# Another order of the steps in all loops of an attention and MLP kernel

## Chip, cores and metric

The kernel runs on one core of a Trainium2 chip, in fp32. The metric is the device time of one execution in microseconds. Engines are named as in the profile: PE (TensorE, matmuls), PEld (its weight loads), DVE (VectorE), ACT (ScalarE), POOL (GpSimd) and SP (SyncE, which here only issues DMAs).

## What is computed

The reference runs a linear attention with a decaying state and feeds its output to an MLP with the exact GELU:

```python
for t in range(S):                                    # S = 768, B = 4, H = 8, head size 48
    cur = einsum('bhd,bhe->bhde', u[None] * kt, vt)
    y[:, :, t] = einsum('bhd,bhde->bhe', rt, state + cur)
    state = wt[:, :, :, None] * state + einsum('bhd,bhe->bhde', kt, vt)
x = y.transpose(0, 2, 1, 3).reshape(3072, 384)
h = x @ w_in                                          # 384 x 2048
g = 0.5 * h * (1.0 + erf(h / sqrt(2)))
out = g @ w_out                                       # 2048 x 384
```

The two weight matrices come in as 64-bit floats; the kernel makes fp32 of them on the chip.

## The kernel before

**Tiling.** The 3072 tokens are cut into eight units of 384 (four batches, two halves each; a second half takes over the state of the first). For each unit the attention gives `xT`, the transposed input of the MLP (three blocks of 128 channels), and the MLP gives 384 rows of the output. Unit 0's attention is done in two parts, of two head pairs each.

**Loops.** Loop x (0 to 7) does the rest of the attention of unit x, begins that of unit x+1, and does the MLP of unit x-1; loop 8 is the last MLP alone. All parts are Python generators that issue a few instructions per step. `PLAN[x]` is a string; each letter advances one generator by one step (L1255). When the string is used up, what is left of the generators is run to its end in a fixed order (L1257). So PLAN is the order in which every engine gets its instructions, and each engine takes its own in that order. The generators:

- `.` the products of the MLP (loop 0: the attention of unit 0's first part; loop 1: `first_mlp`, L1045, with plain matmuls, 16 of h, each followed by a gelu on ACT at L1053, and then the output);
- `s` the attention of unit x from where it was left (loop 0: unit 0's second part), `f` the first steps of the attention of unit x+1;
- `l` loads (SP): the next unit's r, k, w in nine parts and v; in loop 0 the first weight pieces W0 to W2 and the shares of unit 1's input;
- `x` the 11 sums of blocks of xT (`sums_of_x`, DVE, L1036) that the fast product needs; in loop 0 two groups of three warm-up matmuls that keep PE busy (`keep_warm`, L349);
- `v` merges of product results (POOL's accumulating DMAs, L1115, or DVE, L1117 and L1120), `g` the gelus (ACT, L1133), `o` the 30 sums behind the output products (DVE, L1161 to L1168), `e` their 12 copies (ACT, L1084);
- `c` the conversion of one of 16 weight pieces, in four steps: prepare (three ACT operations, L457, L458, L460; two pieces ahead), shift (DVE, L469), nothing, add (DVE, L473) with the load of the piece three further on; `p` (loop 0) prepare for W1 and W2 apart; `w` the load of v for unit 1 (loop 0) and sums of weight blocks (loops 1 and 2); `y` sums of output weights (loop 1).

**The MLP (units 1 to 7)** makes both of its products by a scheme of 20 block products. The first is 2 x 20 steps of the list `STEPS` ("P3", "P12 se", ...; four matmuls each, L1040, with copies by ACT), the second 20 steps of two slots (`OUT_STEPS`). A step of the first list that opens a bank must wait until that bank is free. P17, the third of a loop, opens the bank (m0) that the previous MLP's accumulator D has left; D's last use is the sum "D-00", the last of the 30 in `OUT_SUMS`. The sums before it are A+10, A-00, N5-11, N5+10, M11N5, N4+12. In front of step O17 of the output stands the copy e11 (ACT), the last of `OUT_COPIES`.

**The attention of units 2 to 7** is 43 steps: the products ruk of r, u and k (DVE, L512); transposed sums TTR (L499); the running totals of w, tot (L532: the first two in one step, the rest in the next); products `apart` (L506) and `times` (L540); copies `plain` (ACT, L678) and `lay_out` (DVE, L683, L684); then per level (4 and 16) three bursts of 64x64 matmuls on PE (L708, the fine ones of level 4 at L700), here called d4.0 to d4.2 and d16.0 to d16.2, whose results are copied off the bank pairs by DVE (level 4, L737) or ACT (level 16, six copies, L724), with two bank pairs for three bursts; products of r and k (L753 to L764); the transposes trK (DVE, L657) with 12 DMAs on SP (L652), copies kt (ACT, L806), kv on PE (L822), the states st (DVE, L837), `inside` on PE (L863), a one-column copy named fence (DVE, L875) that PE waits for, y on PE (L908), the copy ysb (L934) with six DMAs, and six copies xT (ACT, L931). Units 0 and 1 use an older form of the middle part with six levels (`halves`, L590): bursts at L573 (level 1 with an additional one, diag), updates (DVE, L615 to L626), copies (DVE, L637, or for levels 16 and 32 ACT, L634), transposes ktT (L796), and products ru of r and u on ACT (L522). Unit 0's first part copies y straight into xT (L915, two copies on ACT, two on DVE).

The order stands in the code as these strings; the kernel has no planner and no due times.

Of the kernel before, what the change touches and what calls it, by code (L numbers as in the profile page):

```python
# [36 lines left out]
NC_SP = 8  # L37
HALFWAY = 2
PLAN = {
    0: ".xll.s...lcsl.ssslsslsls.l.slll..scls.ls.cpc.ss..csss..sscsl.sc...lsc.ssss.ls.l...sf.wfxpf",  # L40
    1: (
        "cl.c.cls.cccss.ccccwccwwc.sw.cccccsclcss.cc.llsscsc.cwccscs.cclsc.ccwscssw.c.wsscc.ccws.cl"
        "lcwwlcwwwsccw.cccsccs.cfcfcc..cl...fc.cfxcx..x.y..f.w....f.x.wy.y.wf.yw.yxy.xx...xywyw...."
        "yxyxwff.wxy"
    ),
    2: (
        ".l..w.wsw.sws..wv...ws..wvv..w.www.vlswwsg.wg..v.swsswswws.wlg..wl..g.s.wgv.vsvswv....ggwv"
        "s..g.vssvvssw..w.ssw.vvg.vvggs.g.vsggogg..eos.w..es..o..osso..eoo.e.o.ooooos..ewwle....eeo"
        "..soo.eo.esl..l.s.ooosoel..oeolslsw....fo.f.ooo.fox.oxxoxxxxxfxfxfx"
    ),  # L50
    3: (
        "....v.s....s....vvg.s.vs.vl.gs....g.s...ls.vg..sss.s.ssv.gs.vsgvs.svvv.vsg.ls.lgv.v.vvs.sg"
        "..gsggsv.gsg..sgg.eo.os..esos..so..oo.loe.eol.o..o.sooeoe..ee....oosesooss..lsel.l.ooosfes"
        "..o..folo.e.f.o.ox..oooxx..oxxxoxfxfxfxx"
    ),
    4: (
        ".ls.s......v..l.g.v..v...sg...vvl.g.v.s.sss..g.svss.vsss...s.ss.vvgvgvsg.glsg..vgss.vvv.v."
        "s.slv.sg.s.ggsglgog.s.e.o.s.eos....os.soooo.eoe....ooeooe...ee.o..sso.e.eoo.lss.lo.l.soeof"
        "sol..oefs..o..o.ofo..oofx.oxxoxxxxxfxfxx"
    ),  # L60
    5: (
        ".s.l..sv....s....v.sg..v..vg..vsl..lg.gvs.v.s..v.sss.vgsgss..s.gsvg.sv.lgssv..s.gs.v.vvv.s"
        ".sv.gvsgsggglgs..oos..es.e...o..os.l.sso.eoeo.s.oo.eeooo.o..e.eo.o..s.oo.sslee.osl.lof..se"
        "os..fl.ooeo..o.fofoo....xoxxooxxxfxxfxfxx"
    ),
    6: (
        "........s..vv......vg.sgs.v..gv..ssv.sv...s..sssvgss..vg.ssslvs.vg.s.vvg.sgl.gs.vv..vsvlgl"
        "s..gssggvsg..gog.s..eeo.s...o.ossso..ee...oooloeo.eolo..s.eo.o.oe..s.oe.o.elss..sooelo.lfs"
        ".o.eoflos....o.ofoof.oxo.x.xoxxxfxxfxfxx"
    ),  # L70
    7: (
        "ss......s.v...v..v.....g.vss...gvvg...s..v.gssg.gsssvs...s..vsgv.svggsvss..vs...vvgs.svvg."
        "ssg.gvsggg..ooesss....oeo.s.os..eo.e..oo.oooeo.oe....se.e.o.oes.oos...ess.osoeos...o.oo.e."
        "o.oo.ox.x.ooxxx.xoxxxxx"
    ),
    8: (
        "...........vv...vv.g..vvg.v..g....gv..v.vggg....gv....v.g.vg.vgvg.vgvv.g.g.g...o.eoe....oo"
        "..e.e...eooooeo....ooe.ooe..oo.oe..o..eoo..oo..oee....ooo.oo.o..oo"
    ),
}  # L80

# [1244 lines left out]
```

## Time and profile before

| | |
|---|---|
| time before, median of 3 runs | 589.58 us (588.73 to 589.81) |
| the profiled execution | 589.16 us |
| its span in the trace | 587.4 us, PE's granted clock 0.996 |
| PE, DVE, ACT, POOL busy | 555.5, 490.4, 330.8, 103.0 us |
| first matmul step of loops 1 to 8 | 49.2, 128.3, 192.9, 260.2, 327.9, 397.1, 462.6, 530.8 us |

In rows of the timeline the columns are: start in us, length in us, engine, line, operation, output and input tiles, shape, number of instructions taken together, and in brackets the idle time of the engine before it with what ended it. "issue" is idle time for which the trace shows no wait. In rows of waits the columns are the sum in us, how often, and the longest. Units are written as the loops: "loop 3" begins at 192.9 us. The trace's times start at the first instruction of the span.

### The profile page before, as it was taken

To read this page: it belongs to the slowest core of one execution; us is meant where nothing else is said; L and a number is where in the kernel's file an instruction comes from. 1 tells how busy PE (TensorE), PEld (TensorE's weight loads), DVE (VectorE), ACT (ScalarE), POOL (GpSimd) and SP (SyncE) were. 2 spreads that over 40 slices of the span, in tenths; PEclk is the share of its full clock that TensorE was granted. 3 is DMA by queue.
4 is the path that set the end of the run, shared out by engine and by line. 5 is a ranking of instruction groups with operands and counts; after the bars stand their busy time and mean duration, and the time that the engine had idled before them with its cause. 6 is when DMAs were issued, how large, how long until landed. Compare 5 with 4: busy or idle time off the path is not lost. (4 is left out here: it accounts for less than half of the span.)

```text
span 587.4 us, 17679 instructions
## 1 busy us (share of the span) xinstructions
PE 555.5 (95%) x7410; PEld 491.5 (84%) x7424; DVE 490.4 (83%) x997; ACT 330.8 (56%) x733; POOL 103.0 (18%) x99
## 2 busy tenths in 40 slices
PE   6769999999999999999998999989999899999997
PEld 3556666569999888999898889979899898989997
DVE  5959989998998989899897989789897989855464
ACT  2348999117862568437762577526772477625820
POOL 3100000005400351006400162003700072000000
PEclk8999999999999999999999999999999999999999
DMA  7829933126723583537813494327824375201001
GB/s 242 265 60 309 353 112 120 41 77 111 103 47 130 135 121 44 130 101 141 138 34 104 119 144 55 68 72 175 122 37 121 95 104 66 42 14 40 1 1 40
DMA packets 71646, 62.15 MB, mean 106 GB/s; under 512 B 32912, under 2 KB 56720, under 8 KB 71568
## 3 DMA queue, kind: packets, MB, share of 16 engines
q1 hardware_dynamic: 50256, 45.62, 25.7%
q0 software_dynamic: 21216, 15.34, 20.0%
q8 instruction: 58, 0.95, 0.7%
q14 instruction: 20, 0.16, 0.1%
q10 hardware_dynamic: 96, 0.07, 0.1%
HBM read 36.24 MB, written 4.72 MB: 70 GB/s over the span
## 5 line engine op out<-in xcount | busy, mean ns | idle before, releaser
L1115 POOL DMA_DIRECT2D g<-o_sb x78 | 95.0, 1504 | 378.5 <-ACT g L1084 312.5
L1164 DVE TENSOR_TENSOR g<-g 128x512 f32<-128x512 f32 x112 | 74.4, 686 | 21.8 <-PE o_ps L1040 19.2
L1084 ACT COPY o_sb<-u_ps 128x384 f32<-128x384 f32 (+1 forms) x56 | 25.6, 457 | 61.0 <-PE u_ps L1040 57.9
L1040 PE MATMUL h_ps<-forms_x,w_in_sb 128*128 128x192 f32 x280 | 58.0, 332 | 0.3 <-ACT g L1084 0.3
L1084 ACT COPY g<-h_ps 128x384 f32<-128x384 f32 x84 | 40.1, 479 | 18.5 <-PE h_ps L1040 16.7
L1040 PE MATMUL o_ps<-w_out_sb,g 128*128 128x192 f32 x280 | 50.1, 326 | 0.0
L1040 PEld LDWEIGHTS h_ps<-forms_x,w_in_sb 128*128 128x128 f32 x280 | 46.5, 190 | 3.1 <-ACT g L1084 2.1
L1133 ACT ACTIVATE g<-g 128x384 f32<-128x384 f32 x98 | 47.0, 521 | 0.7 <-DMA g<-o_sb 0.4
L1040 PEld LDWEIGHTS o_ps<-w_out_sb,g 128*128 128x128 f32 x280 | 46.1, 190 | 0.1
L1040 PE MATMUL o_ps<-t,g 128*128 128x192 f32 x224 | 41.4, 328 | 0.0
L724 ACT COPY a_sb<-d 32x320 f32<-32x320 f32 (+5 forms) x108 | 39.1, 362 | 3.2 <-DVE a_sb L782 1.0
L1040 PE MATMUL h_ps<-forms_x,s 128*128 128x192 f32 x168 | 36.1, 338 | 3.4 <-DVE o_sb L1167 3.3
L1040 PEld LDWEIGHTS o_ps<-t,g 128*128 128x128 f32 x224 | 36.8, 190 | 0.3
L1040 PE MATMUL h_ps<-xT,w_in_sb 128*128 128x192 f32 x168 | 35.0, 331 | 0.0
L1040 PEld LDWEIGHTS h_ps<-forms_x,s 128*128 128x128 f32 x168 | 27.4, 189 | 7.7 <-DVE o_sb L1167 4.7
L1051 PE MATMUL h_ps<-xT,w_in_sb 128*128 128x384 f32 x96 | 33.1, 495 | 0.2 <-ACT g L1053 0.2
L1040 PE MATMUL u_ps<-xT,w_in_sb 128*128 128x192 f32 x168 | 32.5, 329 | 0.2
L708 PE MATMUL d<-kx,rkw 64*64 64x96 f32 x1152 | 30.7, 247 | 1.8 <-DVE kx L684 1.6
L1040 PE MATMUL u_ps<-w_out_sb,g 128*128 128x192 f32 x168 | 31.1, 333 | 1.2 <-ACT u_ps L1084 1.2
L708 PEld LDWEIGHTS d<-kx,rkw 64*64 64x64 f32 x1152 | 25.3, 133 | 7.4 <-issue 3.6
L1059 PE MATMUL o_ps<-w_out_sb,g 128*128 128x384 f32 x96 | 31.4, 488 | 0.0
L837 DVE SCALAR_TENSOR_TENSOR st<-st,tot_sb,kv_ps 128x48 f32<-128x48 f32 x160 | 29.4, 258 | 1.2 <-PE kv_ps L822 1.1
(169 smaller groups left out, 1191.3 us busy)
## 6 DMA issues: line engine op xcount, KB each, us to landing
g<-o_sb POOLq DMA_DIRECT2D x78, 192.0 KB, 4.0
rkw<-in_rkw_dram SPq DMA_DIRECT2D x54, 256.0 KB, 3.4
raw<-in_w_out_dram SPq DMA_DIRECT2D x8, 768.0 KB, 5.6
v_in<-in_v_dram SPq DMA_DIRECT2D x8, 584.0 KB, 3.9
out_dram<-o_sb SPq DMA_DIRECT2D x24, 192.0 KB, 2.1
raw<-in_w_in_dram SPq DMA_DIRECT2D x5, 768.0 KB, 9.5
rkw<-kx SPq DMA_DIRECT2D x72, 48.0 KB, 2.0
rkw<-in_rkw_dram SPq DMA_DIRECT2D x6, 384.0 KB, 7.1
```

The lines of the kernel that those rows point to most:

```text
L708: nc.tensor.matmul(d[half[p], g, i * 3 * C // 2:(i + 1) * 3 * C // 2], lhsT=kc[half[g], n // NI, n % NI, p], rhs=rx[half[g], 2 * n + p], s ...
L724: nc.scalar.copy(out=at[z, g, first:behind, (a + 1) * h:], in_=d[z, :, :, to] if g == slice(None) else d[z, :, to])
L837: nc.vector.scalar_tensor_tensor(out=stq[:, q, c], in0=stq[:, q, c - 1] if c else b4[:, q, NC - 1], scalar=totq[:, q, c:c + 1], in1=kvs[q ...
L1040: nc.tensor.matmul(o, lhsT=lhsT, rhs=rhs, start=start, stop=True, skip_group_check=True)
L1051: nc.tensor.matmul(h_ps, lhsT=w_in_sb[:, f // FI, j, f % FI * 128:(f % FI + 1) * 128], rhs=xT[:, j, :], start=(j == 0), stop=(j == NJ - 1))
L1059: nc.tensor.matmul(o, lhsT=gs[f // FG][:, f % FG, i * 128:(i + 1) * 128], rhs=w_out_sb[:, f, :], start=(f == 0), stop=(f == NF - 1))
L1084: nc.scalar.copy(out=o, in_=z)
L1115: nc.gpsimd.dma_start(out=o, in_=saved[q, t], accum_op=ALU.add)
L1133: nc.scalar.activation(out=o, in_=z, func=AF.Gelu, scale=MINUS.get(h, 1.0))
L1164: nc.vector.tensor_add(o, o, g_block(what[3:5]))
```

## The change

Only the strings in PLAN change. Each loop keeps the number of every letter, apart from one step of `f` less in loop 0 (one step of `s` more in loop 1), one step of `f` more in loop 4 and one less in loop 5 (with one `s` less in loop 5 and one more in loop 6). In words, as far as it matters here:

- Loop 0: both groups of warm-up matmuls come at the very end (before: the first after the first step, the second at the end). The preparation of W1 comes behind the copies of levels 16 and 32 and kt (ACT); before, ahead of them. W0's shift and add come behind unit 0's level-32 update; before, among the levels. So W3's load comes later, too. The copies L915 come ahead of unit 1's ru and tot; before, behind them. The burst diag of unit 1 comes in loop 1, behind the first product of h; before, ahead of it.
- Loop 1: the conversions, levels of unit 1 and products of h alternate in other places; the gelu of h2 comes behind W4's preparation (before: ahead of it), that of h10 behind the level-16 copies (before: ahead).
- Loops 2 to 7: at the end of each loop fewer `x` steps come ahead of D-00 (loops 2, 4 and 6: one instead of three; loops 3 and 7: three instead of six; loop 5: three as before). In loops 4 and 6 the first two totals of the next unit come ahead of the sums N4+12 and M11N5; before, behind them. In loop 5 ruk of unit 6 comes behind the fence (before: ahead of it; in loops 4 and 6 it stays ahead).
- In loops 4 to 7 d16.2 comes right behind d16.1 and the product step P19 ahead of both; before, P19 and an output step stood between them. In loops 3 and 6 d4.0 comes one product step later.
- In all loops the letters `v`, `g`, `o`, `e` and `l` move by a few places; the order within each letter is the generator's and stays.

The diff (of the loops that aren't shown every line is replaced in the same way):

```diff
-    0: ".xll.s...lcsl.ssslsslsls.l.slll..scls.ls.cpc.ss..csss..sscsl.sc...lsc.ssss.ls.l...sf.wfxpf",
+    0: "l.s....llsl.lssslslss.lc.l.slslls...ssss..lcs.s.s.l.ss..ss..sccs.c.s.llpssslw..cs.ffpccxx",
     1: (
-        "cl.c.cls.cccss.ccccwccwwc.sw.cccccsclcss.cc.llsscsc.cwccscs.cclsc.ccwscssw.c.wsscc.ccws.cl"
-        "lcwwlcwwwsccw.cccsccs.cfcfcc..cl...fc.cfxcx..x.y..f.w....f.x.wy.y.wf.yw.yxy.xx...xywyw...."
-        "yxyxwff.wxy"
+        "l.ccswccclss.cw.l.ccccccscs.c.csscccc.scc.sscwccc.cswcs.wcsccscccls.c.ssc.sclcswcwcc.wcwcc"
+        "sslcw..cwlclwccswclsc.cf.w.cw..ccc.cfw..cfyx....f.x..x.f.yxxf.wxw..y..y...wywyx..xyxf.yw.f"
+        ".wxywxyl.yf."
     ),
...
     4: (
-        ".ls.s......v..l.g.v..v...sg...vvl.g.v.s.sss..g.svss.vsss...s.ss.vvgvgvsg.glsg..vgss.vvv.v."
-        "s.slv.sg.s.ggsglgog.s.e.o.s.eos....os.soooo.eoe....ooeooe...ee.o..sso.e.eoo.lss.lo.l.soeof"
-        "sol..oefs..o..o.ofo..oofx.oxxoxxxxxfxfxx"
+        "ls.....s.ss.v....g....vlv.s.gs.vv..g....sv...s.glssvvgsvslsss..gvs.v.gs.ggss..v.sgv.vv..vv"
+        ".slsggs.svsg.gog.g.s.oss.eo.e.o..o.so..ee..ooo..eoe.o..oosee.s..loo.os.oes.e.so.llsleo.of."
+        "s.o.esolo.f..f.ooo.o.foo..xoxxxxxxxffxfxx"
     ),
     5: (
-        ".s.l..sv....s....v.sg..v..vg..vsl..lg.gvs.v.s..v.sss.vgsgss..s.gsvg.sv.lgssv..s.gs.v.vvv.s"
-        ".sv.gvsgsggglgs..oos..es.e...o..os.l.sso.eoeo.s.oo.eeooo.o..e.eo.o..s.oo.sslee.osl.lof..se"
-        "os..fl.ooeo..o.fofoo....xoxxooxxxfxxfxfxx"
+        ".....sll....v....vv..vsg.vs....ggs.v..vs.ls..g.sv.ssssvs.sl..g.vs.vsvgs.s.ggv.gss..l..vsvv"
+        "vsssvg...ggsggogsg.os.oe.se.l.o..o..o.oe.es.o.oeeo....o..ooseoes..ose.loos.ssell..oo.eossf"
+        "..o..fo.oeof..o..xoo.oxox.oxxlxxxffxfxx"
     ),
...
```

More of the change, by code (lines that the diff above doesn't have):

```diff
@@ L39 @@
 PLAN = {
-    0: ".xll.s...lcsl.ssslsslsls.l.slll..scls.ls.cpc.ss..csss..sscsl.sc...lsc.ssss.ls.l...sf.wfxpf",
+    0: "l.s....llsl.lssslslss.lc.l.slslls...ssss..lcs.s.s.l.ss..ss..sccs.c.s.llpssslw..cs.ffpccxx",
     1: (
-        "cl.c.cls.cccss.ccccwccwwc.sw.cccccsclcss.cc.llsscsc.cwccscs.cclsc.ccwscssw.c.wsscc.ccws.cl"
-        "lcwwlcwwwsccw.cccsccs.cfcfcc..cl...fc.cfxcx..x.y..f.w....f.x.wy.y.wf.yw.yxy.xx...xywyw...."
-        "yxyxwff.wxy"
-    ),
-    2: (
-        ".l..w.wsw.sws..wv...ws..wvv..w.www.vlswwsg.wg..v.swsswswws.wlg..wl..g.s.wgv.vsvswv....ggwv"
-        "s..g.vssvvssw..w.ssw.vvg.vvggs.g.vsggogg..eos.w..es..o..osso..eoo.e.o.ooooos..ewwle....eeo"
-        "..soo.eo.esl..l.s.ooosoel..oeolslsw....fo.f.ooo.fox.oxxoxxxxxfxfxfx"
-    ),
@@ L51 @@
-    3: (
-        "....v.s....s....vvg.s.vs.vl.gs....g.s...ls.vg..sss.s.ssv.gs.vsgvs.svvv.vsg.ls.lgv.v.vvs.sg"
-        "..gsggsv.gsg..sgg.eo.os..esos..so..oo.loe.eol.o..o.sooeoe..ee....oosesooss..lsel.l.ooosfes"
-        "..o..folo.e.f.o.ox..oooxx..oxxxoxfxfxfxx"
-    ),
-    4: (
-        ".ls.s......v..l.g.v..v...sg...vvl.g.v.s.sss..g.svss.vsss...s.ss.vvgvgvsg.glsg..vgss.vvv.v."
-        "s.slv.sg.s.ggsglgog.s.e.o.s.eos....os.soooo.eoe....ooeooe...ee.o..sso.e.eoo.lss.lo.l.soeof"
-        "sol..oefs..o..o.ofo..oofx.oxxoxxxxxfxfxx"
-    ),
@@ L61 @@
-    5: (
-        ".s.l..sv....s....v.sg..v..vg..vsl..lg.gvs.v.s..v.sss.vgsgss..s.gsvg.sv.lgssv..s.gs.v.vvv.s"
-        ".sv.gvsgsggglgs..oos..es.e...o..os.l.sso.eoeo.s.oo.eeooo.o..e.eo.o..s.oo.sslee.osl.lof..se"
-        "os..fl.ooeo..o.fofoo....xoxxooxxxfxxfxfxx"
-    ),
-    6: (
-        "........s..vv......vg.sgs.v..gv..ssv.sv...s..sssvgss..vg.ssslvs.vg.s.vvg.sgl.gs.vv..vsvlgl"
-        "s..gssggvsg..gog.s..eeo.s...o.ossso..ee...oooloeo.eolo..s.eo.o.oe..s.oe.o.elss..sooelo.lfs"
-        ".o.eoflos....o.ofoof.oxo.x.xoxxxfxxfxfxx"
-    ),
@@ L71 @@
-    7: (
-        "ss......s.v...v..v.....g.vss...gvvg...s..v.gssg.gsssvs...s..vsgv.svggsvss..vs...vvgs.svvg."
-        "ssg.gvsggg..ooesss....oeo.s.os..eo.e..oo.oooeo.oe....se.e.o.oes.oos...ess.osoeos...o.oo.e."
-        "o.oo.ox.x.ooxxx.xoxxxxx"
-    ),
-    8: (
-        "...........vv...vv.g..vvg.v..g....gv..v.vggg....gv....v.g.vg.vgvg.vgvv.g.g.g...o.eoe....oo"
-        "..e.e...eooooeo....ooe.ooe..oo.oe..o..eoo..oo..oee....ooo.oo.o..oo"
+        "l.ccswccclss.cw.l.ccccccscs.c.csscccc.scc.sscwccc.cswcs.wcsccscccls.c.ssc.sclcswcwcc.wcwcc"
@@ new lines @@
+        "sslcw..cwlclwccswclsc.cf.w.cw..ccc.cfw..cfyx....f.x..x.f.yxxf.wxw..y..y...wywyx..xyxf.yw.f"
+        ".wxywxyl.yf."
+    ),
+    2: (
+        "s.w..s.w.w.s..w..wswv.w..v.ww.vwv.ssw.swgww.swgsvwv.w.sgwv.wssls..wvsw...wg...g...wvsw.gvl"
+        "s..sgvss...gg.ssvgvw.wvgvgvv.glsgv..gs.og.l.oe.s.wsoeo.s...seooe..l.so.ooe.lewo...o..ooeoe"
+        "..os.eolol.s.se..oo.oew.lsw.ooosles..f.fo.oo.o.fo..xooxxfxxxxxfxfxx"
+    ),
+    3: (
+        ".ls....v..s.sl...g...s.vvs..s..l.vg.gvg....s..l..sv.svss.ssss.g.svssgvlvg.sg..vv.vv.gsv.gv"
+        "s.sggv.gslsvs..g.ogsog.e..s.eoo.....seo.oe.os.eoo.e...oooso.e.e.s.soo.ool.lessseo..oeolssf"
+        "....fooo.e..f.xooxo.o..x.oooxlxxxfxfxfxx"
+    ),
@@ new lines @@
+    6: (
+        "s..sl...v.....v..g..ss.v.lvv...g.gvs..gsv..s.v..s.ssggsssvss..ss.l.vg.s..vg.vvggss..vvvv.."
+        "ssssvggg..g.so.ggsoe...seo...ssols.o.o.eooe...o.e.eo.o.o.e.ooeo..ssl.oos.lsel..eslooo..lef"
+        "s..oes.o.lfo..foo.o.o..fooxoxxxxxffxxxfxx"
+    ),
+    7: (
+        "....sv.......gss.v....vsv..g..sg..vvg..s...s.svsgvsvss.ss.ss.vvgs.v.gsg.vg..svg...vv.ssgsv"
+        "v.gg.g.sgso.gseo..es.....osso..ooo.eeoo..e.eso...oooee...os.soe..oos.se.s.oeosos...oo.e..."
+        "oooo..oxo.oxx.oxxxxxxxx"
+    ),
@@ L79 @@
+    8: (
+        "..........v...v...v.v..g.gggv.v.....vv.....g.gvg....vgv.vvvgvgv..vgg..g.vgo..gge..eo...o.o"
+        ".oo.eoe....oeo.e.o..o.oeeo..oo.eo.o.eo....ooe..o.e.oo.o..o.oo.oo.o"
     ),
```

## Prediction

> **What bounds the kernel now.** I read the page first: its line of busy times and PE's slices (busy tenths, 14.7 us each).
>
> ```profile
> PE 555.5 (95%) x7410; PEld 491.5 (84%) x7424; DVE 490.4 (83%) x997; ACT 330.8 (56%) x733; POOL 103.0 (18%) x99
> PE   6769999999999999999998999989999899999997
> ```
>
> TensorE (PE) is busy 95% of the span of 587.4 us; only slices 1 to 3, the first loop, hold clearly less. No edit changes its number of instructions, so the change can only move the 32 us in which PE is idle (587.4 - 555.5), and what it loses when it changes between kinds of work. The table of 50-us windows (length; PE, PEld, DVE, ACT, POOL busy; clock; DMA share; GB/s) says where those 32 us lie.
>
> ```profile
> 0.00:50.00 50.00, 35.43 (x1176) 26.11 (x1190) 36.80 (x113) 20.20 (x35) 8.00 (x21) 0.97 0.60 191
> 50.00:100.00 50.00, 49.35 (x886) 32.71 (x885) 46.20 (x80) 48.31 (x68) 0.00 (x0) 1.00 0.67 236
> 300.00:350.00 50.00, 46.94 (x589) 44.12 (x589) 41.83 (x90) 24.53 (x60) 10.36 (x9) 1.00 0.52 112
> 550.00:587.00 37.00, 33.87 (x208) 33.27 (x206) 19.40 (x38) 11.70 (x32) 0.00 (x0) 0.99 0.05 16
> ```
>
> 14.6 us are in the first 50 (loop 0 and its wait for the first loads) and 3.1 in the last 37 (mostly the last sums and store). The rest, about 14, lies in loops 2 to 7. Of that the waits of PE from 49 us on name this much:
>
> ```profile
> PE y_ps L908 <- DVE fence L875: 3.4, 4, 1.6
> PE h_ps L1040 <- DVE o_sb L1167: 3.3, 4, 1.1
> PE d L708 <- DVE kx L684: 1.6, 4, 0.6
> PE u_ps L1040 <- ACT u_ps L1084: 1.2, 2, 0.9
> PE kv_ps L822 <- DMA rkw<-kx: 1.0, 1, 1.0
> ```
>
> Each is a place where PE has come, in the order that PLAN fixes, to a step whose input is still queued on another engine behind steps that weren't urgent. Those are what another order can take away, so I price them one by one. In the first window and in the second ACT matters: 48.31 of 50 us busy, with the conversion of the weights.
>
> **Loop boundaries (P17).** Step P17, the third of a loop, needs the bank that D-00, the last of the 30 sums (L1167), gives back. PE's waits there:
>
> ```profile
> 195.36 0.92 PE L1040 MATMUL h_ps<-forms_x,s 128*128 128x192 f32 x4 [0.62 <-DVE o_sb L1167]
> 262.20 0.76 PE L1040 MATMUL h_ps<-forms_x,s 128*128 128x192 f32 x3 [0.56 <-DVE o_sb L1167]
> 330.46 0.92 PE L1040 MATMUL h_ps<-forms_x,s 128*128 128x192 f32 x4 [1.05 <-DVE o_sb L1167]
> 465.18 0.92 PE L1040 MATMUL h_ps<-forms_x,s 128*128 128x192 f32 x4 [1.03 <-DVE o_sb L1167]
> ```
>
> The sum is 3.26. Ahead of D-00 DVE does this in the third of them:
>
> ```profile
> 325.42 0.37 DVE L1161 TENSOR_TENSOR u_ps<-u_ps,o_sb 128x192 f32<-128x192 f32 x1 [0.89 <-PE u_ps L1040]
> 325.69 0.95 DVE L532 TENSOR_TENSOR tot_sb<-rkw 128x768 f32<-128x768 f32 x1
> 326.68 0.56 DVE L532 TENSOR_TENSOR tot_sb<-tot_sb 128x384 f32<-128x384 f32 x1
> 328.98 0.36 DVE L1036 TENSOR_TENSOR forms_x<-xT 128x192 f32<-128x192 f32 x1
> 330.06 0.34 DVE L1167 TENSOR_TENSOR o_sb<-o_sb,o_ps 128x192 f32<-128x192 f32 x1
> ```
>
> It idles 0.89 us for PE (first row) and only then does the two totals of the next unit (0.95 and 0.56 us, L532), which depend on no PE step. D-00 is the sum at 330.06. In the new order the totals stand ahead of the two sums N4+12 and M11N5 (at the boundaries from loop 4 to 5, this one, and from 6 to 7), so they fall into that idle time, and of the sums of x (L1036, 0.36 us in the fourth row) two fewer stand ahead of D-00, from loop 3 to 4 three fewer. Idle filled, 0.9, and two sums, 0.7, are more than the 1.05 and 1.03 waited; the 0.62 and 0.56 go by the two and three sums of x alone. I take all four as gone: **-3.26**. From 5 to 6, where PE now doesn't wait, four products ruk (L512) move from ahead of the fence to behind it: +0.3, an estimate (bounds 0 and 1.05, the largest of the rows above). In all **-2.96**. What is late next is the first burst of the loop, priced as unchanged below.
>
> **First bursts (d4.0).** Their input is DVE's L684.
>
> ```profile
> 213.65 1.88 PE L708 MATMUL d<-kx,rkw 64*64 64x96 f32 x80 [0.58 <-DVE kx L684]
> ```
>
> In loop 3 (first row; two bursts are taken together in it) the burst moves one PE step (0.65) later: **-0.5**. In loop 6 it does, too, but there ruk has moved behind the fence and DVE comes later by about as much; in loops 4, 5 and 7 it keeps its place, and PE and DVE come sooner by about the same. So the 1.0 left of the 1.6 stays. If DVE's idle isn't filled, the boundary waits come back here (first rival).
>
> **Loop 5's fence, and e11.**
>
> ```profile
> 384.62 3.03 DVE L512 SCALAR_TENSOR_TENSOR kx<-rkw,u_sb,rkw 128x384 f32<-128x384 f32 x4
> 387.72 0.99 PE L908 MATMUL y_ps<-rkw,st 64*64 64x64 f32 x51 [1.57 <-DVE fence L875]
> 393.11 1.08 PE L1040 MATMUL u_ps<-w_out_sb,g 128*128 128x192 f32 x5 [0.94 <-ACT u_ps L1084]
> ```
>
> In loop 5 the products (first row, 3.03 us) stand between the states and the fence, and PE waits 1.57 for it (second row). They move behind the fence; I leave 0.2 for the fence itself: **-1.37**. In loops 4 and 6 they stay ahead of it, so the rest of the 3.4 stays. y sooner makes its copy ysb and the six copies xT on ACT (L931) sooner; the copy e11, queued behind them, made PE wait 0.94 (third row). I leave 0.3: **-0.64** (bounds 0 and 0.94).
>
> **The wait for kv in loop 4.**
>
> ```profile
> 311.66 0.86 PE L822 MATMUL kv_ps<-v_in,rkw 64*64 64x48 f32 x44 [0.95 <-DMA rkw<-kx]
> ```
>
> Twelve DMAs that SP issues turn trK's results round for kv; the chain has next to no slack in any loop, and PE waits in this one alone. The new order keeps the chain and its place. I take no gain (bounds: 0.95 gained; 0.95 lost in another loop).
>
> **A new wait (d16.2).** In loops 4 to 7 the third burst of level 16 now comes right behind the second, d16.1, with the step P19 ahead of both, and it needs the pair of banks that six copies of ACT (L724) empty. In loop 4 of before:
>
> ```profile
> 291.42 2.59 ACT L724 COPY a_sb<-d 32x320 f32<-32x320 f32 x6 [0.17 <-DVE a_sb L782]
> 291.96 1.05 PE L708 MATMUL d<-kx,rkw 64*64 64x96 f32 x40
> 292.95 0.92 PE L1040 MATMUL h_ps<-xT,w_in_sb 128*128 128x192 f32 x4
> ```
>
> The copies end at 294.01. d16.1 (second row) takes 0.99 up to the next step, P19 (third row) about 0.75; with these two changed round d16.2 is due at 291.96 + 0.75 + 0.99 = 293.70. That is a wait of 0.3, and with the copies' release I take 0.35 per loop, **+1.4**. Bounds: 0, if the copies follow PE's earlier start; 0.7, if ACT is just in another copy (0.36 more) when they are due. Queued behind the waiting burst are PE's products, and behind these DVE's sums.
>
> **Fewer changes of work on PE.** Four matmuls of a product step begin every 0.65 us. After a burst it is more:
>
> ```profile
> 226.89 0.92 PE L1040 MATMUL h_ps<-xT,w_in_sb 128*128 128x192 f32 x4
> 227.64 0.85 PE L1040 MATMUL u_ps<-rkw,g 128*128 128x192 f32 x4
> 228.42 0.56 PE L708 MATMUL d<-kx,rkw 64*64 64x96 f32 x16
> ```
>
> From 226.89 to 227.64 are 0.75, from there to 228.42 0.78: 0.10 and 0.13 more. Counting the groups in PLAN there are six fewer such changes in loops 1 to 7 (102 before, 96 after); by 0.12 each that is **-0.7**, bounds 0 and 1.2.
>
> **Loops 0 and 1.** The path to loop 1 runs through DVE, ACT and PE:
>
> ```profile
> 24.28 0.55 DVE L469 TENSOR_SCALAR f<-f 128x768 uint32<-128x768 uint32 x1
> 27.41 0.95 DVE L473 CUSTOM_DVE_ANT_0 w_in_sb<-f,e 128x1536 uint16<-128x1536 uint16 x1
> 27.21 0.93 ACT L457 ACTIVATE f<-raw 128x768 f32<-128x768 f32 x1 [7.95 <-DMA raw<-in_w_in_dram]
> 28.05 0.98 ACT L458 ACTIVATE e<-raw,two 128x768 f32<-128x768 uint32 x1
> 29.06 1.06 ACT L460 ACTIVATE e<-raw 128x768 f16<-128x768 f32 x1
> 45.08 2.13 ACT L522 ACTIVATE kx<-rkw,u_sb 128x384 f32<-128x384 f32 x4 [2.25 <-issue]
> 49.20 1.24 PE L1051 MATMUL h_ps<-xT,w_in_sb 128*128 128x384 f32 x3
> 55.21 1.70 PE L573 MATMUL d<-rkw 64*64 64x32 f32 x96
> 31.24 0.38 PE L349 MATMUL warm<-zeros 128*128 128x512 bf16 x1 [2.72 <-issue]
> ```
>
> W0's shift and add (0.55 + 0.95 = 1.5) leave the middle of DVE's work for unit 0; the three operations that prepare W1 (2.97, by the next three rows) leave the place ahead of the level-16 copies; the copies of xT come ahead of ACT's L522 (2.13) instead of behind it. Together the first product (49.20) can begin up to 1.5 + 2.13 = 3.6 sooner. Against it, the burst diag (of the size of a burst of this unit, the last row but one: 1.70) now comes behind that product, and both groups of warm-up matmuls (3 x 0.38 = 1.14) stand ahead of it: -3.6 + 1.7 + 1.1 = -0.8. In loop 1 ACT has 48.31 of 50 us of work; gelu 2 comes behind the three operations that prepare a weight (2.97) instead of ahead of them, gelu 10 behind the level-16 copies of A1. I take +0.8 for this, and so **0** for both loops; bounds: a gain of 1.9 (no late gelu, and the warm-ups in time in which PE waits anyway: 3.6 - 1.7), a loss as in the second rival. The 2.72 of the last row, PE ready and held by nothing that the trace names, sits in the first window, in which the DMA engines are busy 0.60 of the time, so a load moved (W3's, 768 KB, issued by W0's add) can move it either way. The Trainium skill, "Runtime: NRT & Kernel Launch", section "Instruction fetch mechanics", says that instructions are fetched sequentially ahead and the fetch mostly hidden; by it such a hole would not be a fetch that loads delay, and the sum stays as it is. No run here shows which.
>
> The letters l and v move too: SP's loads, issued behind or ahead of a move of trK, and POOL's accumulating DMAs (L1115). POOL is busy 103.0 us of 587.4, and a merge by a step or two earlier or later lies beside PE's products; I cost both at nothing. Without that cover it is one late gelu or one late kv, which is the 0.95 of the row at 311.66.
>
> **Sum.** -2.96 - 0.5 - 1.37 - 0.64 + 1.4 - 0.7 + 0 = -4.77. The profiled execution took 589.16 us, 0.4 below the median of 589.58; the terms are differences, so I set them against the median: 589.58 - 4.77 = **584.8 us**. If the bounds of the new wait, of kv, and of loops 0 and 1 all fell well it would be 584.8 - 1.4 - 0.95 - 1.9 = 580.6.
>
> **Rivals.**
> First, **DVE stays the bound** from the fence to the first burst. It is busy 44 us or so of 50 throughout (the windows have 41.83 in the slackest), and what it does between fence and L684 is the same work. Where its idle (0.89) isn't filled, the time not waited at P17 is waited at d4.0: the 2.96 goes, 587.8. For it speaks that the row of 0.58 in loop 3 comes behind a P17 wait already; against it that DVE's idle is in the trace and tot needs nothing from PE.
>
> Second, **ACT in loop 1 makes it slower.** It has 1.7 us to spare in 50. PE needs the bank that a gelu empties; where a gelu stands behind work that stood behind it before, PE waits up to that work. There are two such places, gelu 2 and gelu 10, and each is bounded by one preparation (2.97): 5.9 in all, and 589.6 - 4.8 + 5.9 = 590.7. It decides from a loss of 4.8 on. For it speaks the 48.31; against it that the sum of ACT's work in this loop is the same, and that two more banks stand between PE and the late gelu.
>
> Third, the **order moves waits and saves nothing**: each removed wait has a new one of its size at another step (the zero-slack chain of kv in three loops, 0.95 each; d16.2 at 0.7 each, 1.4 more): 584.8 + 2.9 + 1.4 = 589.1.
>
> **How the numbers follow.** About 0.2%, 1.2 us, is what a measurement of this kernel can tell from no change: 588.4 to 590.8 counts as the same. Chances: the forecast 0.47 (its own range 582.5 to 587), better than that 0.05, first rival 0.16, second 0.19, third 0.13. Faster are the first two and half of the first rival (0.08): 0.60. Same are its other half and 0.05 of the third: 0.13. Slower are the second, most of which ends above 590.8 where the gains of the other loops come in part only, and 0.08 of the third: 0.27. The range reaches from the best case, 580.6, to 592, the second rival with a little of the gain of 4.8 missing: what it leaves out, below and above, is under 2 in 10.
>
> **What would show it.** Right: the four P17 waits gone and D-00 ending before PE gets there; y in loop 5 waiting less than 0.3; the first product of loop 1 at 46 to 49; small waits of d16.2 on L724. Wrong: P17's waits found again before d4.0 in loops 3 to 7 (first rival); PE waits on L1053 or on ACT copies between 50 and 105 us, and loop 2 beginning later than 128.3 (second); waits for DMA at kv in more than one loop (third).

## The result and the profile after

The changed kernel takes 583.77 us (median of 4 runs, 582.83 to 584.98); the kernel before, with a fourth run, 589.69 (588.73 to 593.72). The ratio is 0.9888, with a 95% interval of 0.9839 to 0.9937: faster by 1.1%. The forecast was 584.8. Total and direction came out; where the time came from did so only in part, as the traces and experiments below show.

The profiled execution of the changed kernel took 584.98 us, the longest of its four, with a span of 583.2. From its page, engines and PE's slices:

```profile
PE 557.0 (96%) x7410; PEld 492.4 (84%) x7424; DVE 491.9 (84%) x997; ACT 330.3 (57%) x733; POOL 103.1 (18%) x99
PE   6889999999999999999999999999999999999997
```

The work is the same. PE's second and third slice went from 7 and 6 to 8 and 8. Three of the 50-us windows (length; PE, PEld, DVE, ACT, POOL busy; clock; DMA share; GB/s):

```profile
0.00:50.00 50.00, 39.88 (x1188) 29.15 (x1202) 39.08 (x117) 23.14 (x39) 8.02 (x21) 1.00 0.67 210
50.00:100.00 50.00, 48.27 (x883) 31.58 (x882) 45.82 (x78) 48.37 (x68) 0.00 (x0) 1.00 0.61 219
300.00:350.00 50.00, 48.83 (x645) 46.10 (x644) 44.50 (x93) 26.54 (x66) 12.91 (x11) 1.00 0.60 125
```

PE gained 4.5 us of work in the first 50 us (39.88 for 35.43) and 1.9 in the window at 300. The first is what the prediction had put at nothing. The waits of PE from 49 us on (sum, times, longest):

```profile
PE y_ps L908 <- DVE fence L875: 2.4, 5, 0.8
PE d L708 <- ACT a_sb L724: 1.5, 4, 0.4
PE y_ps L908 <- issue: 1.5, 2, 0.8
PE u_ps L1040 <- DVE g L1120: 1.1, 2, 0.6
PE h_ps L1051 <- ACT g L1053: 1.0, 1, 1.0
PE o_ps L1040 <- DVE g L1164: 0.8, 2, 0.6
PE h_ps L1040 <- ACT g L1084: 0.7, 2, 0.4
PE d L708 <- DVE kx L684: 0.5, 2, 0.4
PE u_ps L1040 <- ACT u_ps L1084: 0.5, 2, 0.3
```

The 3.3 us on the sums L1167 (P17) are gone from the list. New are d16.2's waits on L724, four of them, and waits of output steps for DVE (L1120, L1164). The kernel before hadn't these last in this trace, but its second trace has two for L1120, of 1.46 and 1.50 us; they are explained below, under "A merge that comes early or late". Four single rows, of P17 in loop 5, of y and e11's step in loop 5, and of d16.2:

```profile
325.32 0.92 PE L1040 MATMUL h_ps<-forms_x,s 128*128 128x192 f32 x4
382.23 0.99 PE L908 MATMUL y_ps<-rkw,st 64*64 64x64 f32 x52 [0.17 <-DVE fence L875]
387.55 0.76 PE L1040 MATMUL u_ps<-w_out_sb,g 128*128 128x192 f32 x3 [0.18 <-ACT u_ps L1084]
291.28 0.56 PE L708 MATMUL d<-kx,rkw 64*64 64x96 f32 x16 [0.38 <-ACT a_sb L724]
```

P17 had waited 1.05, y 1.57, e11's step 0.94; they wait 0, 0.17 and 0.18.

Executions of one order differ by several us (586.2 to 593.3 in twelve of the kernel before), so a single us is read from the lengths of loops in traces, not from times. A loop's length here is the distance between two starts of P17 on PE. Mean over the traces of each order, with the number of traces; the old order's include those of the experiments that have it in that loop:

| loop | old order | new order | difference | forecast |
|---|---|---|---|---|
| 0 and 1, up to P17 of loop 2 | 130.0 (3) | 127.0 (6) | -3.0 | 0 |
| 2 | 66.0 (7) | 65.2 (4) | -0.8 | -0.6 |
| 3 | 66.9 | 66.8 | -0.1 | -1.1 |
| 4 | 67.3 | 66.4 | -0.9 | -0.7 |
| 5 | 68.3 | 67.1 | -1.2 | -1.4 |
| 6 | 66.9 | 66.8 | -0.1 | -0.7 |
| 7 | 68.2 | 68.2 | 0.0 | +0.35 |
| 8 | 55.2 | 55.1 | -0.1 | 0 |

The forecasts are the prediction's terms laid to their loops, without its -0.7 for changes of work. The sum measured is -6.2, of which -3.2 are in loops 2 to 8 and -3.0 in the first two.

**A merge that comes early or late.** Loops 5 and 7 scatter by 1 to 3 us within each order, loop 3 by under 0.4. The place is the same in all traces, about 30 us behind P17: DVE's merge L1120 needs a block of `g` to which one of POOL's accumulating DMAs (L1115, 192 KB, issued 25 us behind P17) adds. From issue to landing this DMA took 4.1 to 4.5 us or 5.2 to 5.8 in the traces, never between. Loop 7 in the first and second trace of the kernel before, on DVE, and then PE in the second:

```profile
494.62 0.55 DVE L1120 TENSOR_TENSOR g<-g,u_ps 128x384 f32<-128x384 f32 x1 [0.27 <-DMA g<-o_sb]
498.34 0.56 DVE L1120 TENSOR_TENSOR g<-g,u_ps 128x384 f32<-128x384 f32 x1 [1.80 <-DMA g<-o_sb]
500.55 0.92 PE L1040 MATMUL u_ps<-rkw,g 128*128 128x192 f32 x4 [1.50 <-DVE g L1120]
```

Laid apart by this DMA, the loops of the table read otherwise (differences taken before rounding):

| loop, DMA | old order (traces) | new order (traces) | difference |
|---|---|---|---|
| 5, early | 68.0 (5) | 66.3 (1) | -1.6 |
| 5, late | 69.2 (2) | 67.3 (3) | -1.9 |
| 7, early | 66.8 (2) | 67.1 (1) | +0.3 |
| 7, late | 68.7 (5) | 68.5 (3) | -0.2 |

So the change gained more in loop 5 than the mean of -1.2 shows, and in loop 7 the spread covers what it did. What makes the DMA late isn't shown; it is late in either order.

### The profile page after: what moved, and what is told of

It reads as the page before. It is cut to its first block, busy times and chain, and to the rows that moved or that the text cites. A ratio compares the mean times of both kernels' runs of the same rounds, so it can differ in the third digit from the quotient of the medians.

```text
span 583.2 us, 17698 instructions
## 1 busy us (share of the span) xinstructions
PE 557.0 (96%) x7410; PEld 492.4 (84%) x7424; DVE 491.9 (84%) x997; ACT 330.3 (57%) x733; POOL 103.1 (18%) x99
## 5 line engine op out<-in xcount | busy, mean ns | idle before, releaser
L1115 POOL DMA_DIRECT2D g<-o_sb x78 | 95.1, 1504 | 373.5 <-ACT g L1084 273.0
L1164 DVE TENSOR_TENSOR g<-g 128x512 f32<-128x512 f32 x112 | 75.1, 687 | 20.4 <-PE o_ps L1040 17.2
L724 ACT COPY a_sb<-d 32x320 f32<-32x320 f32 (+5 forms) x108 | 39.1, 362 | 4.1 <-PE h_ps L1040 1.5
L573 PEld LDWEIGHTS d<-rkw 64*64 64x64 f32 x1152 | 20.3, 141 | 13.1 <-issue 7.1
```

The source lines that it names most:

```text
L573: nc.tensor.matmul(d[half[p], g, n * width:(n + 1) * width], lhsT=kc[half[g], b, i, p], rhs=right(half[g], b, i, p), start=True, stop=True)
L724: nc.scalar.copy(out=at[z, g, first:behind, (a + 1) * h:], in_=d[z, :, :, to] if g == slice(None) else d[z, :, to])
L1115: nc.gpsimd.dma_start(out=o, in_=saved[q, t], accum_op=ALU.add)
L1164: nc.vector.tensor_add(o, o, g_block(what[3:5]))
```

## The experiments

Two theories. **A** is the prediction: the gain comes from waits of PE in loops 2 to 7, each worth its length; loops 0 and 1 give nothing, being set by the order of DVE's and ACT's work. **B**: in loops 2 to 7 DVE sets the pace of most of a loop, so that PE's won time is partly waited elsewhere; and in loop 0 the gain comes from the loads: one load less competes with the fetch of PE's instructions. From here on a hole is idle time of PE for which the trace names no wait ("issue").

### The halves, and both kernels again

The two orders were combined, written short:

```diff
-PLAN = {0: before, 1: before, 2..8: before}
+PLAN = {0: after,  1: after,  2..8: before}    # e1_loops01
+PLAN = {0: before, 1: before, 2..8: after}     # e2_loops28
```

New order in loops 0 and 1 only. 

> The new order in loops 0 and 1 alone, the old order in loops 2 to 8. By the prediction's sum (these two loops give nothing, loops 2 to 7 give 4.8 us) it takes 589.6 us. By the reading of the two traces (the first product of loop 2 begins 2.9 us sooner, loops 2 to 8 give 1.3) it takes 586.8 us.

New order in loops 2 to 8 only. 

> The old order in loops 0 and 1, the new one in loops 2 to 8. By the prediction's sum 584.8 us; by the reading of the two traces 588.3 us, with a step of -1.2 us at kv of loop 4 and at the starts of loops 5 and 7, and losses at d16.2 and at the merges of loops 5 and 7.

The changed kernel again. 

> The changed kernel once more, for its spread and a second trace. If the holes named issue in loop 0 (0.86, 0.27 and 0.80 us, 4.2 us in the kernel before) are set by the order, they come back with about these sizes; if they are chance, they move by a us or more. Time 583 to 585 us.

The kernel before again. 

> The kernel before once more, for a second trace. If the holes of 2.72 and 1.49 us in loop 0 are set by the order of the loads, they come back at the same places; if they are chance, loop 1 begins up to 4 us sooner than at 49.2 in this trace and the change's gain in loop 0 is partly chance. Time 588.7 to 590 us.

All beside 590.05 us of the kernel before: e1 588.09 (ratio 0.996, 0.993 to 0.999), e2 588.02 (0.9958, 0.9927 to 0.9989), r_after 583.53 (0.9882, 0.9835 to 0.9928), r_before 589.60 (0.9979, 0.9948 to 1.0009). Each half gives about 0.4%. Theory A had one half give nothing and the other all, ratios of 1 and 0.992; both lie outside the intervals. The other reading, from the first two traces (2.9 and 1.3 us), lies inside both. The halves together give 0.8% where the whole gives 1.2%; the intervals are too wide to say that more than the sum is there.

The second trace of the kernel before has the hole of 2.72 us again (the row below; it stood at 31.24 in the first), and holes at the same places as the first, though not all of the same size (0.34 us for 1.49, 2.10 for 0.42). In the second trace of the changed kernel the holes did not keep their sizes: 1.28 us for 0.80, none for 0.27, and one of 1.30 where the first had none. So a hole's place is fixed and its size in part chance.

```profile
30.81 0.59 PE L349 MATMUL warm<-zeros 128*128 128x512 bf16 x1 [2.72 <-issue]
```

Counting PE's recorded instructions, weight loads included, this matmul is number 1208 in both traces; the other large holes behind number 700 are at 701, 954, 1717, 2228, 5812 and 14259. In the traces of the old order that have 14 more records they are, not all in every trace, at 705, 961, 1217, 1729, 2241, 3265, 5826 and 14273: 961, 1217, 1729, 2241, 3265 and 14273 are 705 plus whole multiples of 256, and 5826 is one more than such. Holes at a fixed count of instructions, whatever the instruction, point to the fetch of the next block. The trace's list of DMA packets shows the block itself: single packets of 16384 bytes on the instruction queue q8: 58 of them, where PE's 15001 recorded instructions make 58.6 blocks of 256. In the kernel before one of them starts at 28.97 us and takes 0.89; PE had issued the end of its block at 28.5 and went on at 31.24. In all five traces with this hole PE goes on 1.36 to 1.49 us after the packet's end.

### What loop 0's gain comes from

Three edits to the kernel before, each with one part of the new order of loop 0, and one to the changed kernel. In the cut below the first line is the old one for all three; e9 and e5 have the `weight_in` edit of e4, too, and all three a stream `h` that issues W3's load:

```diff
 # e3_prep_late: W1's preparation (p) behind the copies, W1's shift behind that
-    0: ".xll.s...lcsl.ssslsslsls.l.slll..scls.ls.cpc.ss..csss..sscsl.sc...lsc.ssss.ls.l...sf.wfxpf",
+    0: ".xll.s...lcsl.ssslsslsls.l.slll..scls.ls.cc.ss..csss..sscsl.s...ls.pssss.ls.l...sf.wfxccpf",
 # e9_conv_late: all steps of c from W0's shift on behind the transposes; h issues W3's load where it was
+    0: ".xll.s...lcsl.ssslsslsls.l.slll..scls.ls.p.ss..hsss..sssl.s...ls.ccccccssss.ls.l...sf.wfxpf",
 # e4_w3_late: h issues W3's load behind the transposes; none with W0's add
+    0: ".xll.s...lcsl.ssslsslsls.l.slll..scls.ls.cpc.ss..csss..sscsl.sc...lsc.hssss.ls.l...sf.wfxpf",
-        for _ in weight_in(i + 3):
+        for _ in weight_in(i + 3 if i else len(pieces)):
 # e5_w3_early: the same two lines on the changed kernel, h behind the 15th dot
```

> The kernel before; only W1's preparation on ACT (and its shift on DVE) comes behind the copies of levels 16 and 32 of unit 0, as in the new order; W0's shift and add and W3's load stay early. If ACT's queue sets the time of loop 0 (the prediction's reading: 2.97 us out of the way of the level-16 copies), PE's hole of 1.6 to 2.7 us ahead of the last level-32 burst goes and h0 begins 1.5 to 2.7 us sooner than in the three traces of the old order (48.6 to 50.7). If the hole is the fetch of PE's instructions held up by W3's load, it stays, and h0 begins at 48 to 50.

> The kernel before; only the load of W3 (768 KB) is issued later, behind the first part's transposes, as in the new order, instead of with W0's add. If a load in flight lengthens the fetch, the hole ahead of the last level-32 burst (PE's 1208th instruction) falls from 1.6 to 2.7 to under 0.5 us, perhaps with ACT's level-16 copies as the next limit, and h0 begins at 46.5 to 48.5. If ACT's order sets it, nothing changes (48.6 to 50.7).

> The changed kernel; only the load of W3 is issued early, at the place in loop 0 that it had before. Fetch held up by the load: a hole of 1 to 2.7 us at PE's 1207th instruction, where the changed kernel has 0 to 0.27, and h0 at 44.5 to 46.5 instead of 43.3. ACT's order: h0 stays at 43.3.

> The kernel before; in loop 0 the conversions of W0 and W1 on DVE (shift 0.55, add 0.95 us) come behind the first part's transposes, as in the new order, while W1's preparation on ACT and the issue of W3's load stay where they were. By the prediction's step (1.5 us out of the middle of DVE's work) h0 begins 1.5 us sooner than the old order's 48.6 to 50.7, at 47 to 49. If the hole ahead of the last level-32 burst covers that, it stays at 1.6 to 2.7 us and h0 begins at 48.6 to 50.7.

The load's place once more. 

> The kernel before with W3's load issued later, once more, for a second trace: the hole at PE's 1217th instruction under 0.5 us and h0 at 45 to 47.5 if the load's place does it; a hole of over 1.5 us there and h0 at 48.6 or later if the first trace was chance.

| | hole at 1208 (1217) | first product of loop 1 (us) | P17 of loop 2 (us) |
|---|---|---|---|
| old order, 3 traces | 2.72, 2.72, 1.62 | 49.2, 50.7, 48.6 | 129.7, 131.1, 129.3 |
| e3_prep_late | 2.17 | 49.0 | 129.9 |
| e9_conv_late | 1.35 | 49.3 | 130.1 |
| e4_w3_late, e4_again | none, none | 45.7, 46.5 | 126.1, 126.9 |
| e5_w3_early | none | 43.2 | 126.0 |
| new order (after, r_after) | 0.27, none | 43.3, 43.4 | 126.8, 125.6 |

With ACT's or DVE's part alone the first product and P17 stay where the old order has them. The place of one load of 768 KB brings, in the traces, all that loops 0 and 1 gain by P17 of loop 2. The start of these times varies by a us or two; counted from PE's entry into the block before the hole, the first product comes 23.2 to 26.0 us later in the five traces with W3 in its old place (e2's among them) and 20.9 and 21.9 in e4's two. In e4_again PE passes the place without a hole:

```profile
27.20 0.93 PE L573 MATMUL d<-rkw 64*64 64x64 f32 x48
28.11 0.59 PE L349 MATMUL warm<-zeros 128*128 128x512 bf16 x2
28.63 0.93 PE L573 MATMUL d<-rkw 64*64 64x64 f32 x48
```

The DMA view of the two us from 25 to 27 says why. In the kernel before, all packets are data:

```profile
DMA packets 383, 0.75 MB, mean 377 GB/s; under 512 B 44, under 2 KB 44, under 8 KB 383
```

In e4_again, in the same window:

```profile
DMA packets 154, 0.31 MB, mean 155 GB/s; under 512 B 25, under 2 KB 25, under 8 KB 153
q8 instruction: 1, 0.02, 2.7%
```

PE enters the block before at 25.04 us in the one and 24.65 in the other. The next block's packet starts at 28.97 in the one, behind W3's load, which SP issued at 24.32 and which landed at 30.41, and at 25.86 in the other, where W3 is issued at 33.22. Taking PE's entry into the block before as the moment of the request, the fetch began after 3.9 us in the one and 1.2 in the other. In all five traces that have W3 issued ahead of that entry it is 2.6 to 3.9 us, in the six others that show the entry 1.0 to 1.2. So the fetch waits behind data that was queued before it.

e5 **missed**: its W3 load, though in loop 0's place of before, was issued at 26.54, after the fetch of that block (25.48), and nothing happened. So it isn't that a load is in flight when PE arrives, as the expectation had it, but that it was issued ahead of the fetch. By time e5 gives 582.28 us (0.9863 of the kernel before, 0.9829 to 0.9896), the same as the changed kernel.

In times, loops 0 and 1 give less than in the traces: e4 588.95 and 588.02 beside 590.07 and 588.90 (ratios 0.9975, 0.9950 to 1.0001, and 0.9984, 0.9956 to 1.0012), e3 589.36 (0.9987) and e9 590.32 (1.0028, 1.0002 to 1.0054). The traced execution of e4_w3_late is the fastest of its ten, 4.2 us below their median, and that of r_before the slowest of its twelve. That W3's load is the cause is shown for the traced executions; for e4's untraced ones the differences have the same sign, but both intervals reach 1.

### Whether PE's waits are worth their length

P19 back between d16.1 and d16.2, loops 4 to 7 (here loop 5's place):

```diff
-  .l..vsvvvsssv
+  .l.vs.vvvsssv
```

> The changed kernel; in loops 4 to 7 the step P19 goes back between d16.1 and d16.2. If each wait of PE is worth its length, the four waits of 0.39 us on L724 go and loops 4 to 7 get 0.4 to 0.6 us shorter each, 1.5 to 2 us in all. If DVE's merges and sums set the output phase, the waits go and steps of the output wait for L1120 and L1164 in their place: loops 4 to 7 get shorter by under 0.5 us in all.

In loops 4 and 6 the products ruk come behind the fence (here loop 4's place):

```diff
-  o.of.s.o.es
+  o.o.sf.o.es
```

> The changed kernel; in loops 4 and 6 the four products ruk of the next unit come behind the fence, as they do in its loop 5. If each wait of PE is worth its length, the two waits of y of 0.80 us go and the time falls by 1.6 us, loops 4 and 6 by 0.8 each. If DVE sets the pace from the fence to the next first burst, ruk's 3 us are only moved, P17 or the first burst of loops 5 and 7 waits for them instead, and loops 4 to 7 together are shorter by under 0.5 us.

The copies of the finest level's results left out:

```diff
-                        nc.vector.copy_predicated(out=at[:, g].rearrange("p n (m b) -> p n m b", b=FINE),
-                                                  mask=mask.to_broadcast(data.shape), data=data)
                         yield
```

> The changed kernel; left out are the copies of the finest level's results (L782, two per unit 2 to 7, 1.92 us of DVE per loop). If DVE sets the output phase of loops 3 to 7, the waits of PE for L1120 and L1164 and the many holes of 0.1 to 0.2 us ahead of output steps go, and loops 3 to 7 get shorter by 0.5 to 1.5 us each, 3 to 6 in all. If PE's own work sets them, they stay within 0.2 us each and the time within 1 us of the changed kernel's.

Lengths of the loops:

| loop | changed (after, r_after, e5) | e6 | e7 | e8 |
|---|---|---|---|---|
| 3 | 66.9, 66.9, 66.7 | 67.0 | 67.0 | 66.1 |
| 4 | 66.3, 66.6, 65.8 | 66.2 | 67.5 | 65.8 |
| 5 | 67.5, 66.3, 67.3 | 66.2 | 67.3 | 66.4 |
| 6 | 66.6, 66.4, 66.5 | 66.7 | 67.7 | 66.0 |
| 7 | 68.6, 68.2, 67.1 | 68.2 | 68.8 | 68.3 |

**e6**: d16.2's waits fall from 0.39 to 0.19 each, and loops 4 to 7 take 267.4 us together, where the changed kernel took 269.1, 267.5 and 266.6. r_after, with the merge early and late in the same loops as e6, is the nearest: 0.2 us. No gain can be told; time 583.17 (0.9886, 0.9848 to 0.9923).

**e7** is the clearest. Both waits of 0.80 at the fence are gone, and loops 4 and 6 are 1.3 and 1.2 us longer than the mean of the three traces, not 0.8 shorter; the time is 587.92 beside 590.13 (0.9964, 0.9935 to 0.9993), a good part of the change's gain lost, more than the 2.5 us of the two loops. (e2 has the new order in these loops, too: 66.8 and 67.6. Its loop 6 holds a wait for ACT of 1.55 us, which e7's has at 0.38.) At the end of loop 4 of e7, PE and then DVE:

```profile
323.80 1.54 PE L1040 MATMUL u_ps<-xT,w_in_sb 128*128 128x192 f32 x8 [1.19 <-DVE o_sb L1167]
325.83 0.92 PE L1040 MATMUL h_ps<-forms_x,s 128*128 128x192 f32 x4 [0.49 <-DVE o_sb L1167]
```

```profile
315.48 2.34 DVE L512 SCALAR_TENSOR_TENSOR kx<-rkw,u_sb 128x384 f32<-128x384 f32 x3
319.24 1.77 DVE L499 TRANSPOSE_TENSOR_REDUCE rkw<-kx 128x48 f32<-128x1536 f32 x1
325.43 0.35 DVE L1167 TENSOR_TENSOR o_sb<-o_sb,o_ps 128x192 f32<-128x192 f32 x1
```

ruk now runs behind the fence (first DVE row), and the sums that free banks for the next loop, the last at 325.43, end too late for PE by 1.19 and again 0.49. DVE is busy without a gap from one to the other. At the fence, DVE in the changed kernel and then in e7:

```profile
314.14 3.03 DVE L512 SCALAR_TENSOR_TENSOR kx<-rkw,u_sb 128x384 f32<-128x384 f32 x4
316.99 0.22 DVE L875 COPY fence<-y_ps 128x2 f32<-128x2 f32 x2
314.37 0.16 DVE L875 COPY fence<-y_ps 128x2 f32<-128x2 f32 x1 [0.55 <-PE y_ps L863]
314.74 3.08 DVE L512 SCALAR_TENSOR_TENSOR kx<-rkw,u_sb 128x384 f32<-128x384 f32 x4 [0.21 <-issue]
```

In the changed kernel PE waits 0.79 for ruk at the fence, and then for nothing until P17, while DVE doesn't wait there at all. In e7 the fence comes first, and DVE waits 0.55 us for PE's `inside`, and 0.21 more for which the trace names no wait, before it begins ruk. Counted from the loop's P17, ruk begins 1.3 us later and the last of the sums ends 1.3 later, which is the loss. So ruk ahead of the fence fills time in which DVE would have waited for PE.

**e8** leaves out 1.92 us of DVE's work per loop. Against the means of the three traces loops 3 to 6 get 0.7, 0.5, 0.7 and 0.5 us shorter, loop 7 by nothing: 2.4 in all, under the 3 that B had asked for but above A's 0.2 each. Not all of it is DVE's work: in loop 5 the merge was early in e8, and late in two of the three traces; r_after, early too, has 66.3 beside e8's 66.4. In loop 4 e5 is as short as e8 (65.8). What is left clear of the spread is 0.7 in loop 3 and 0.5 in loop 6. d16.2's waits in loops 4 to 7 fell from 0.39 to 0.12, too, since ACT's copies of level 16 wait for those of the finest level. The time, 583.72 beside 590.13 (0.9896, 0.9862 to 0.9929), doesn't tell it from the changed kernel's. So DVE's work sets a part of loops 3 and 6; that it sets the pace of loops 4, 5 and 7, as B had it, isn't shown.

## Why the prediction was right, and where it was not

- **P17** (-3.26): right as waits, all four went. The +0.3 at the start of loop 6 did not come. But the wait of 1.03 at the end of loop 6 brought next to nothing for that loop (-0.1): its four traces of the new order have a wait of 0.33 to 1.55 us for ACT in its first product, 15 us behind P17, that no trace of the old order has. In the second trace of the changed kernel, ACT and then PE:

```profile
405.04 0.48 ACT L1084 COPY o_sb<-u_ps 128x384 f32<-128x384 f32 x1 [1.05 <-DMA g<-o_sb]
405.42 0.53 ACT L1133 ACTIVATE g<-g 128x384 f32<-128x384 f32 x1
405.84 0.48 ACT L1084 COPY u_ps<-h_ps 128x384 f32<-128x384 f32 x1
406.38 0.92 PE L1040 MATMUL h_ps<-forms_x,s 128*128 128x192 f32 x4 [0.53 <-ACT u_ps L1084]
```

  ACT waits at this place for an accumulating DMA in the old order as well (0.97 in the second trace of before), but the new order puts a gelu (second row) between that wait and the copy that PE needs. That is a price of the moved letter `g`, which the prediction's sum doesn't have.
- **d4.0 in loop 3** (-0.5) and P17 at its end (-0.56): the waits went, but the loop is only 0.1 shorter. What came in their place lies in pieces that the idle column hardly shows: in the second trace of the changed kernel

```profile
222.19 0.92 PE L1040 MATMUL h_ps<-xT,w_in_sb 128*128 128x192 f32 x4
223.14 0.92 PE L1040 MATMUL u_ps<-rkw,g 128*128 128x192 f32 x4
```

  the second step begins 0.95 us after the first, where the prediction's rows of 226.89 and 227.64 had 0.75. Four steps of the output are late in this way, by 0.18 to 0.30 us each against the second trace of before, and add up to 0.96, the second matmul of each step included; the first waits for DVE (L1120), the other three for ACT. In e8 the same pair stands 0.75 apart again:

```profile
223.86 0.92 PE L1040 MATMUL h_ps<-xT,w_in_sb 128*128 128x192 f32 x4
224.61 0.81 PE L1040 MATMUL u_ps<-rkw,g 128*128 128x192 f32 x4
```

  With less of DVE's work two of the four are gone, and the loop is 0.7 shorter. So a part of it is the first rival's mechanism, DVE as the bound, but in the output phase instead of at d4.0; the rest is ACT's. The failed step is to count each of these two waits at its length: PE came to the output 0.5 us sooner, and the results of DVE and ACT that the output steps need did not.
- **Loop 5's y and e11** (-2.01): the waits fell by 1.40 and 0.76, as forecast; the loop by 1.2 in the mean, and by 1.6 to 1.9 where the merge was alike.
- **kv of loop 4** (0, with 0.95 as a bound): right. The wait was in one trace of seven of the old order (68.3 us for that loop, 67.1 in the six others).
- **d16.2** (+1.4): 0.38, 0.39, 0.39, 0.39. Right as a wait; by e6, taking half of it away gives nothing that can be told.
- **The letters l and v** (0, "lies beside PE's products"): whether the merge L1120 is late moves loops 5 and 7 by 1 to 2 us, in both orders. That the change makes it late more often can't be told from these traces. The prediction's reason for costing POOL's DMAs at nothing doesn't hold at this place.
- **Fewer changes of work** (-0.7): not measured by itself, and not visible: PE's busy time rose by 1.5 us.
- **Loops 0 and 1** (0): the largest miss, -3.0. The step's reasons, DVE's 1.5 us and ACT's order, don't move the first product when changed alone (e3, e9). The prediction had the hole of 2.72 in its rows, named the load that could move it, and then left it at nothing. The page of the Trainium skill that it weighed there, "Runtime: NRT & Kernel Launch", section "Instruction fetch mechanics", describes blocks of 256 instructions fetched ahead, in 16 KiB pieces, and the traces agree with both figures. It calls the fetch mostly hidden; here it cost 1.4 to 2.7 us at one block where a load was queued ahead of it, and the measurement decides.
- **The second rival** (ACT in loop 1): one wait for a gelu of 0.99 us, at 52.34, of the 5.9 us bounded. Not what decides.

So the total was right in part by luck, because two errors cancelled: in the traces loops 2 to 8 gave 3.2 us where 4.8 had been forecast (too much in loops 3 and 6 and for changes of work), and the first two gave 3.0 where nothing had been.

## What to carry to other kernels

A wait of the bounding engine is worth its length only if the engine that it waits for has slack behind it; where that engine is busy without a gap up to the next place where the two meet, the wait moves there, as e7's did, with a loss because the moved work had filled a wait of that engine's own. Before adding up waits, follow the second engine from one meeting to the next. And where large loads run beside an engine with thousands of instructions, look for idle time named "issue" at a fixed count of instructions: the remedy here was the place of a load, not the order of the work. Where a loop's length falls in two groups over traces of one kernel, look for the transfer that does it before comparing means.

## What was not expected of the hardware

- PE's instructions come in blocks of 256 as single packets of 16384 bytes, on a queue of the DMA engines that carry the data. Counted from PE's entry into the block before, one packet began after 1.0 to 1.2 us with no load of 768 KB issued ahead of it and after 2.6 to 3.9 us behind one; PE's hole there was at most 0.27 us and 1.35 to 2.72.
- One accumulating DMA of 192 KB took 4.1 to 4.5 us or 5.2 to 5.8 from issue to landing at the same place of the same kernel; DVE waited 0.3 us or 1.3 to 1.8 for it (e8, with less of DVE's work, aside).
- A step that is late by under 0.17 us shows no idle time, since a matmul is drawn 0.33 us long while the next of a run begins 0.163 after it. Such a step also delays the second of its four matmuls by 0.10 us. Comparing starts shows such delays where the idle column doesn't.
